# Six pairs of seven products instead of five, and bank sums put in front at a block's end

## The chip, the core and the metric

The kernel runs on one core of a Trainium2 chip. The metric is the device time of one execution in microseconds (us), the median over runs. The profile is of one execution. The engines are TensorE (PE, with its weight load PEld), VectorE (DVE), ScalarE (ACT), GpSimd (POOL) and SyncE (SP), whose queue issues the transfers used here.

## The reference

Attention with a local mask for four heads and a strided mask for four, over 8 batches of 576 tokens, gives x of 4608 tokens x 512. Then:

```python
h = x @ w_in            # 512 -> 2048
g = h * np.cos(h)
return (g @ w_out).astype(np.float32)   # 2048 -> 512
```

All is float32. The kernel multiplies in the type fp32r: each factor is split into a rounded high part and the low part that is left, and a product takes three matmuls (high x high, high x low, low x high).

## The kernel before

The first half of the time goes to attention and to h, batch by batch, where h is written to DRAM as `h_all`. The change is in the second half, the output stage. It works through 18 blocks of 256 tokens (`s`), and in each through 8 pairs (`f`) of 128-row slices of w_out. One step of the stage is a pair (s, f): `gate` makes the factors of the pair from h, and `Outputs.pair` multiplies them with the weights into banks of PSUM.

A pair is multiplied in one of two ways. A plain pair takes four products of 128 x 128 by 512 columns, 12 matmuls. A pair of seven takes seven products of 128 x 128 by 256 columns in Strassen's manner, 21 matmuls; for it the gate is extended by sums (`g[:, 4]` to `g[:, 7]`) and the weights by sums made beforehand (`output_sums`, `split_sums`). `SEVEN` lists the pairs of seven, of which block 1 uses only the first three (the length of `SUMMED`); block 0 is all plain, and so is the last block before. `ROWS` names the pairs whose weights lie in the tiles laid out for whole rows of 512 columns.

A gate goes through these steps: load h (`h_in`, from SP's queue); ScalarE writes k to `wave` (PSUM) and VectorE the remainder `r` (line 655); ScalarE takes the sine (line 657) and VectorE the product with h (line 664 or 673); for a pair of seven GpSimd then makes three sums (lines 674, 675, 678); ScalarE casts the high part `g_hi` (line 183), and `rest`, GpSimd or VectorE, subtracts it to give the low part `g_lo` (line 184). `LEADS` says how many pairs ahead of its multiplication each step of a plain pair or of a pair of seven is emitted. `BY_VECTOR` names the plain pairs whose low part VectorE makes; their product is written back to `wave`, so that one input of the subtraction lies in PSUM. For the other plain pairs the product goes to `r` in SBUF, and GpSimd subtracts. All of GpSimd's instructions for gates are chained in the order of the pairs (`by_gpsimd`).

Pairs of seven gather parts that the two halves of the output share in the banks `more` and `most`. After the last pair of seven, `shared` copies one half of `more` on ScalarE (line 746) and forms the sums on VectorE (lines 747, 749, 752), in two steps behind pairs 6 and 7. `store` adds them to the banks `lower` and `upper` (line 761; in blocks without pairs of seven it copies, line 768) and sends the rows out. Five banks are used in turn. The order of the instructions on each engine is otherwise written down by a planner from its own estimates; `order` adds a constraint of order without a wait.

Of the kernel before, what the change touches and what calls it, by code (L numbers as in the profile page):

```python
# [13 lines left out]
F32 = mybir.dt.float32  # L14
# [4 lines left out]
AF = mybir.ActivationFunctionType  # L19
ALU = mybir.AluOpType  # L20
# [6 lines left out]
P = 128  # L27
# [52 lines left out]

TB = 2 * P
NTB = NTOK // TB
SEVEN = (4, 5, 6, 1, 2)
ROWS = (0, 3, 7)


LEADS = ((6, 4, 3, 2), (7, 4.5, 3.5, 2))
AHEAD = tuple(PER_BATCH - n for n in (20, 17, 13, 10, 7, 3))

BY_VECTOR = (0, 3, 7)  # L90


SUMMED = (14, 28, 36)
# [9 lines left out]
def attention_cos_ffn(ctx, tc, qkl, vl, qkvs, w_in, w_out, eye, eye16, mask_l0, mask_l, mask_s, out):  # L103
    nc = tc.nc
# [18 lines left out]
    w_all = dram.tile([NFC, P, DM], F32, name="w_all")  # L123
    t_all = dram.tile([len(SEVEN), P, 2 * DM], F32, name="t_all")

# [8 lines left out]
    def order(later, first, reason):  # L134
        tc.add_manual_dep(
            later.ins, first.ins.name,
            mybir.DependencyInfo(mybir.DependencyClass.NoSync, mybir.DependencyReason.DATA), reason=reason,
        )
# [12 lines left out]
    def with_product(begun):  # L151
        if turn is not None:
            order(begun, turn, "with this product")

    def weight_tile(f):
        pool, n = (by_rows, len(ROWS)) if f in ROWS else (wp, NF - len(ROWS))
        return pool.tile([P, 2, 2, 2 * P], F32R, name="w", bufs=2 * n)
# [8 lines left out]
    def to_float32(raw, out, bits=None):  # L166
# [12 lines left out]
            out=out, in0=top, scalar=3, in1=bits, op0=ALU.logical_shift_left, op1=ALU.bitwise_or  # L179
        )  # L180

    def split(x, hi, lo, cast=nc.scalar.copy, rest=nc.gpsimd):
        with_product(cast(out=hi, in_=x))  # L183
        return rest.tensor_tensor(out=lo, in0=x, in1=hi.bitcast(F32), op=ALU.subtract)  # L184

    wi, whole = [], []

# [410 lines left out]
    def output_sums(cv, n):  # L598

        f = SEVEN[n]  # L600
        both = whole_tile(cv).rearrange("p (f n) -> p f n", f=2)
# [12 lines left out]
    def split_sums(room, n):  # L614
# [6 lines left out]
        split(t[:, :3], most[:, 0], most[:, 1])  # L621
        sums[SEVEN[n]] = [(most[:, 0, n], most[:, 1, n]) for n in range(3)]
        yield
# [3 lines left out]
        split(t[:, 3], *last)  # L627
        sums[SEVEN[n]].append(last)
        yield
# [1 line left out]
    wo, lasts, gates, sums = [], [], {}, {}  # L631

    def seven(s, f):
        return 0 < s < NTB - 1 and f in SEVEN[:len(SUMMED) if s == 1 else len(SEVEN)]

    of_gates = []

    def by_gpsimd(begun):
        if of_gates:
            order(begun, of_gates[-1], "pair by pair")  # L640
        of_gates.append(begun)

    def gate(s, f):

        h = hp.tile([P, 2 * TB], F32, name="h_in")
        nc.sync.dma_start(
            out=h.rearrange("p (f t) -> p f t", f=2),
            in_=h_all[2 * f:2 * f + 2, :, s * TB:(s + 1) * TB].rearrange("f p t -> p f t"),
        )
        yield  # L650
        r = rp.tile([P, 2 * TB], F32, name="r")
        wave = sg.tile([P, 2 * TB], F32, name="wave")
        k = wave.bitcast(I32)
        with_product(nc.scalar.activation(out=k, in_=h, func=AF.Copy, scale=1.0 / (2.0 * math.pi), bias=0.25))  # L654
        nc.vector.scalar_tensor_tensor(out=r, in0=k, scalar=-2.0 * math.pi, in1=h, op0=ALU.mult, op1=ALU.add)  # L655
        yield
        sin = nc.scalar.activation(out=wave, in_=r, func=AF.Sin, bias=quarter)  # L657
        with_product(sin)
        if s == 0 and f == 0:
            order(sin, exps[-1], "one change of tables")  # L660
        pool = nc.gpsimd
        if not seven(s, f):
            low, pool = (wave, nc.vector) if f in BY_VECTOR else (r, nc.gpsimd)
            nc.vector.tensor_tensor(out=low, in0=wave, in1=h, op=ALU.mult)
            yield
            g_hi, g_lo = (gp.tile([P, 7 * P], F32R, name=name) for name in ("g_hi", "g_lo"))
            lo = split(low, g_hi[:, :4 * P], g_lo[:, :4 * P], rest=pool)
            if pool is nc.gpsimd:
                by_gpsimd(lo)
            gates[s, f] = g_hi, g_lo  # L670
            yield
        g = gs.tile([P, 8, P], F32, name="g")
        nc.vector.tensor_tensor(out=g[:, :4].rearrange("p n t -> p (n t)"), in0=wave, in1=h, op=ALU.mult)
        by_gpsimd(pool.tensor_tensor(out=g[:, 4], in0=g[:, 0], in1=g[:, 2], op=ALU.add))
        by_gpsimd(pool.tensor_tensor(  # L675
            out=g[:, 5:7], in0=g[:, 0:5:4], in1=g[:, 1:2].broadcast_to([P, 2, P]), op=ALU.subtract
        ))
        by_gpsimd(pool.tensor_tensor(out=g[:, 7], in0=g[:, 3], in1=g[:, 6], op=ALU.subtract))  # L678
        yield
        g_hi, g_lo = (gp.tile([P, 7 * P], F32R, name=name) for name in ("g_hi", "g_lo"))  # L680
        by_gpsimd(split(g[:, 1:].rearrange("p n t -> p (n t)"), g_hi, g_lo))
        gates[s, f] = g_hi, g_lo
        yield

# [8 lines left out]
    class Outputs:  # L693
# [48 lines left out]
        def shared(self):  # L742

            more, most = self.banks["more"], self.banks["most"]
            self.t = op.tile([P, 5, 2 * P], F32, name="t")
            with_product(nc.scalar.copy(out=self.t[:, 0], in_=more[:, 0]))
            nc.vector.tensor_tensor(out=self.t[:, 4], in0=more[:, 1], in1=self.t[:, 0], op=ALU.add)
            yield
            nc.vector.tensor_tensor(
                out=self.t[:, 1:3], in0=most, in1=self.t[:, 4:5].broadcast_to([P, 2, 2 * P]), op=ALU.add  # L750
            )
            nc.vector.tensor_tensor(out=self.t[:, 3], in0=most[:, 0], in1=self.t[:, 2], op=ALU.add)
            yield

        def store(self):

            rows = out[self.s * TB:(self.s + 1) * TB, :].rearrange("(h p) d -> h p d", h=2)
            for half, name in enumerate(("lower", "upper")):
                o = op.tile([P, 2, 2 * P], F32, name="o", bufs=4)
                if "more" in self.banks:  # L760
                    nc.vector.tensor_tensor(
                        out=o, in0=self.banks[name], in1=self.t[:, 2 - 2 * half:4 - 2 * half], op=ALU.add
                    )
                parts = (slice(0, 1), slice(1, 2)) if self.last and half else (slice(0, 2),)
                for i, part in enumerate(parts):
                    if "more" not in self.banks:
                        copy = nc.scalar.copy if half == i else nc.vector.tensor_copy
                        copy(out=o[:, part], in_=self.banks[name][:, part])
                    nc.sync.dma_start(
                        out=rows[half].rearrange("p (n d) -> p n d", n=2)[:, part], in_=o[:, part]  # L770
                    )
# [10 lines left out]
    with ExitStack() as phase:  # L782
# [5 lines left out]
        banks = {  # L788
            name: phase.enter_context(
                tc.tile_pool(name=f"ps_{name}", bufs=bufs, space=bass.MemoryType.PSUM, reuse_waits="tile")  # L790
            ) for name, bufs in (("m", 3), ("n", 1), ("o", 1))
        }
# [8 lines left out]
        m, n, o = ((pools[name], name) for name in "mno")  # L801
# [35 lines left out]
        begun = np.interp(range(UNITS, B * UNITS + 3), [k for k, _ in KNOTS], [at for _, at in KNOTS])  # L837
        begun = begun.astype(int).tolist()
        bursts, turns = {}, {}
        waiting = {True: [], False: []}  # L840
        for n, at in enumerate(begun):
            k = n + UNITS
# [11 lines left out]
        for f in range(NF):  # L854
            first = FirstBlock(f)
            for slot in range(STEP):
                plan[STEP * f + slot] = partial(first.products, slot)
        for i, (b, f) in enumerate(itertools.product(range(1, B), range(NF)), NF):
            block = Block(b, f)
# [18 lines left out]
        for n in range(NFC - LATE):  # L878
            at = (B - 1) * PER_BATCH + STEP * (n // 2) + 12 + 3 * (n % 2)
            in_steps(output_weights(lambda: whole_tile(cv)[:, :DM], n), at - 6, at)  # L880
        for n, f in enumerate(SEVEN):
            at = 2 * PER_BATCH + 17 * (2 * f + 2)
# [12 lines left out]
        for slot in range(max(*plan, *steps) + 1):  # L895
# [9 lines left out]
            if b == B - 1:  # L905
                if at == 0:
                    attention.close()
                    sg = ctx.enter_context(tc.tile_pool(
                        name="sg", bufs=3, space=bass.MemoryType.PSUM, side="right", reuse_waits="tile"
# [10 lines left out]

    op = ctx.enter_context(tc.tile_pool(name="op", bufs=2, reuse_waits="tile"))
    tp = ctx.enter_context(tc.tile_pool(name="tp", bufs=1, reuse_waits="tile"))
    gs = ctx.enter_context(tc.tile_pool(name="gs", bufs=3, reuse_waits="tile"))
    pools = {"q": ctx.enter_context(
        tc.tile_pool(name="ps_q", bufs=1, space=bass.MemoryType.PSUM, reuse_waits="tile")
    )}
# [2 lines left out]
    for n in range(NFC - LATE, NFC):  # L929
        rest = nc.vector if n % 2 else nc.gpsimd  # L930
# [8 lines left out]
    for i, (s, f) in enumerate(tiles):  # L939
        if f == 0:  # L940
            block = Outputs(s)
        ahead(i)
        for step in made.get(i, ()):
            next(step, None)
        block.pair(f, *gates.pop((s, f)), partial(ahead, i + 0.5))
        if "more" in block.banks and f >= max(SEVEN):
            if f == max(SEVEN):
                shared = block.shared()
            next(shared, None)
        if f == NF - 1:  # L950
            block.store()

# [93 lines left out]
```

## Time and profile before

| what | value |
|---|---|
| median of 3 runs | 858.97 us (857.16 to 859.54) |
| the profiled execution | 857.26 us, its span 855.5 us |
| granted TensorE clock, mean | 0.998 of 2.4 GHz |
| TensorE busy | 845.1 us, 99% of the span |
| VectorE, ScalarE, GpSimd busy | 66%, 62%, 63% |

The span goes from the first to the last instruction. Busy shares are means over stages with different limits; matmuls are pipelined, so the distance from one start to the next says more than a duration. Line numbers are those of the kernel before.

### The profile page before, as it was taken

To read this page: it belongs to the slowest core of one execution; us is meant where nothing else is said; L and a number is where in the kernel's file an instruction comes from. 1 tells how busy PE (TensorE), PEld (TensorE's weight loads), DVE (VectorE), ACT (ScalarE), POOL (GpSimd) and SP (SyncE) were. 2 spreads that over 40 slices of the span, in tenths; PEclk is the share of its full clock that TensorE was granted. 3 is DMA by queue.
4 is the path that set the end of the run, shared out by engine and by line. 5 is a ranking of instruction groups with operands and counts; after the bars stand their busy time and mean duration, and the time that the engine had idled before them with its cause. 6 is when DMAs were issued, how large, how long until landed. Compare 5 with 4: busy or idle time off the path is not lost.

```text
span 855.5 us, 23160 instructions
## 1 busy us (share of the span) xinstructions
PE 845.1 (99%) x9147; PEld 785.3 (92%) x9147; DVE 567.4 (66%) x1087; ACT 528.4 (62%) x1031; POOL 539.7 (63%) x543
## 2 busy tenths in 40 slices
PE   9999999999999999999999999999999999999998
PEld 5799999999998999999999889999999999999996
DVE  5888755768658567676333667777777677767671
ACT  3766545545445354454456887777777777777772
POOL 2578984416207134162166478999899989898951
PEclk9999999999999999999999999999999999999999
DMA  9698444566666667665456844444444444444330
GB/s 333 189 297 296 145 163 165 178 214 207 224 222 208 230 222 226 227 213 210 155 195 222 280 135 129 131 124 125 129 131 124 132 128 124 134 126 136 120 127 26
DMA packets 91901, 151.82 MB, mean 177 GB/s; under 512 B 8464, under 2 KB 53008, under 8 KB 91792
## 3 DMA queue, kind: packets, MB, share of 16 engines
q1 hardware_dynamic: 91072, 150.11, 53.8%
q8 instruction: 72, 1.18, 0.6%
q14 instruction: 37, 0.30, 0.1%
q10 hardware_dynamic: 720, 0.23, 0.1%
HBM read 96.30 MB, written 54.00 MB: 176 GB/s over the span
## 4 chain that ended last, share of the span: by engine, by line
PE 90%; POOL 3%; ACT 2%; DVE 2%; DMA 1%; issue 1%; DVEq 0%; ACTq 0%; POOLq 0%
PE q L709 44%; PE m L532 19%; PE n L532 9%; PE o L532 5%; PE m L503 4%; PE acc L335 2%; PE acc L400 2%; PE acc L318 2%; POOL x_lo L184 2%; PE acc L387 1%; PE acc L811 1%; PE acc L370 1%; DMA h_all<-h 1%; DMA w_all<-sums 1%; PE m L370 0%
## 5 line engine op out<-in xcount | busy, mean ns | idle before, releaser
L709 PE MATMUL q<-w,g_hi 128*128 128x512 f32 (+1 forms) x1000 | 199.9, 338 | 0.0
L709 PEld LDWEIGHTS q<-w,g_hi 128*128 128x128 f32 x1000 | 159.7, 188 | 22.1
L184 POOL TENSOR_TENSOR g_lo<-g,g_hi 128x896 fp32r<-128x896 f32 x78 | 165.1, 2132 | 6.3 <-ACT g_hi L183 6.0
L709 PE MATMUL q<-w,g_lo 128*128 128x512 f32 (+1 forms) x500 | 111.4, 337 | 0.0
L532 PE MATMUL m<-x_hi,v 128*128 128x288 f32 x448 | 109.4, 299 | 0.8 <-ACT m L540 0.8
L532 PE MATMUL m<-x_hi,w 128*128 128x288 f32 x448 | 108.5, 298 | 0.4 <-DVE h L550 0.4
L655 DVE SCALAR_TENSOR_TENSOR r<-wave,h_in 128x512 f32<-128x512 int32 x144 | 96.1, 685 | 15.2 <-ACT wave L654 13.8
L657 ACT ACTIVATE wave<-r,quarter 128x512 f32<-128x512 f32 x144 | 98.6, 688 | 5.9 <-DVE r L655 5.9
L183 ACT CAST g_hi<-g 128x896 fp32r<-128x896 f32 x78 | 73.4, 941 | 39.6 <-POOL g L678 27.7
L709 PEld LDWEIGHTS q<-w,g_lo 128*128 128x128 f32 x500 | 82.7, 188 | 10.9
L654 ACT ACTIVATE wave<-h_in 128x512 int32<-128x512 f32 x144 | 83.6, 591 | 7.6 <-DVE g_lo L184 7.4
L709 PE MATMUL q<-v,g_hi 128*128 128x256 f32 x624 | 85.4, 279 | 0.0
L532 PEld LDWEIGHTS m<-x_hi,v 128*128 128x128 f32 x448 | 78.1, 188 | 2.1 <-ACT m L540 1.3
L532 PEld LDWEIGHTS m<-x_hi,w 128*128 128x128 f32 x448 | 78.0, 188 | 1.4 <-DVE h L550 0.7
L709 PEld LDWEIGHTS q<-v,g_hi 128*128 128x128 f32 x624 | 78.3, 188 | 0.0
L288 POOL TENSOR_TENSOR pn_s<-e_sb,z 128x324 f32<-128x324 f32 x28 | 20.9, 748 | 90.2 <-DVE z L286 84.0
L184 DVE TENSOR_TENSOR g_lo<-wave,g_hi 128x512 fp32r<-128x512 f32 x54 | 37.2, 689 | 53.2 <-PE q L709 36.0
L540 ACT COPY m<-m 128x288 f32<-128x288 f32 x112 | 44.5, 397 | 43.7 <-PE m L532 37.0
L288 POOL TENSOR_TENSOR e_sb<-e_sb,z 128x384 f32<-128x384 f32 x24 | 20.3, 844 | 77.6 <-DVE z L286 77.2
L532 PE MATMUL m<-x_lo,v 128*128 128x288 f32 x224 | 66.1, 295 | 0.0
L532 PE MATMUL m<-x_lo,w 128*128 128x288 f32 x224 | 65.9, 294 | 0.0
L675 POOL TENSOR_TENSOR g<-g 128x256 f32<-128x256 f32 x78 | 57.7, 740 | 6.1
(137 smaller groups left out, 2051.8 us busy)
## 6 DMA issues: line engine op xcount, KB each, us to landing
h_all<-h SPq DMA_DIRECT2D x128, 288.0 KB, 2.9
h_in<-h_all SPq DMA_DIRECT2D x144, 256.0 KB, 2.8
qk<-in_qkvs SPq DMA_DIRECT2D x28, 324.0 KB, 4.4
out<-o SPq DMA_DIRECT2D x35, 256.0 KB, 3.0
qk<-in_qkl SPq DMA_DIRECT2D x21, 416.0 KB, 4.4
raw<-in_w_in SPq DMA_DIRECT2D x16, 512.0 KB, 5.3
raw<-in_w_out SPq DMA_DIRECT2D x16, 512.0 KB, 4.8
v<-in_vl SPq DMA_DIRECT2D x24, 224.0 KB, 4.0
```

The source lines that it names most:

```text
L183: with_product(cast(out=hi, in_=x))
L184: return rest.tensor_tensor(out=lo, in0=x, in1=hi.bitcast(F32), op=ALU.subtract)
L288: nc.gpsimd.tensor_tensor(out=pn, in0=e, in1=z[:, :n].unsqueeze(2).broadcast_to([P, n, w]), op=ALU.mult)
L318: self.scored = self.pe(nc.tensor.matmul(s_ps[quarter_of(c), t * KW:(t + 1) * KW], q_t[half(j), p, QB * t:QB * (t + 1)], k_t[half(j), p, Q ...
L503: in_turn(nc.tensor.matmul(self.banks[i, j], a[:, c * P:(c + 1) * P], y[:, c], start=k == 0 and m == 0, stop=k == 1 and m == len(ops) - 1, ...
L532: in_turn(nc.tensor.matmul(bank, a[:, c * P:(c + 1) * P], y[:, c], start=first and i == 0, stop=i == len(ops) - 1, skip_group_check=True,))
L540: nc.scalar.copy(out=t, in_=self.bank[name[0]])
L654: with_product(nc.scalar.activation(out=k, in_=h, func=AF.Copy, scale=1.0 / (2.0 * math.pi), bias=0.25))
L655: nc.vector.scalar_tensor_tensor(out=r, in0=k, scalar=-2.0 * math.pi, in1=h, op0=ALU.mult, op1=ALU.add)
L657: sin = nc.scalar.activation(out=wave, in_=r, func=AF.Sin, bias=quarter)
L675: by_gpsimd(pool.tensor_tensor(out=g[:, 5:7], in0=g[:, 0:5:4], in1=g[:, 1:2].broadcast_to([P, 2, P]), op=ALU.subtract))
L709: in_turn(nc.tensor.matmul(at, a, w, start=first, stop=True, skip_group_check=True))
```

## The change

Pair 3 joins `SEVEN`, which has then six of eight pairs, and leaves `ROWS`; the last block uses pairs of seven as well. `BY_VECTOR` becomes (1, 3, 4, 6) and holds for pairs of seven too: of the six, VectorE makes the low parts of 1, 3, 4 and 6 from `g` and `g_hi`, GpSimd those of 2 and 5. The plain pairs 0 and 7 give their low parts to GpSimd. The three sums of each pair of seven stay on GpSimd. The leads of pairs of seven grow from (7, 4.5, 3.5, 2) to (8, 5.5, 4.5, 2), and `g` gets a fourth buffer. `shared` emits its copy and all its sums behind the last pair of seven (pair 6), and `then` holds every later k, sine, cast, remainder, product and VectorE low part of a gate behind them on its engine. `store` adds in parts, so that the last block can send its last half in two.

```diff
-SEVEN = (4, 5, 6, 1, 2)
-ROWS = (0, 3, 7)
+SEVEN = (4, 5, 6, 1, 2, 3)
+ROWS = (0, 7)
-LEADS = ((6, 4, 3, 2), (7, 4.5, 3.5, 2))
+LEADS = ((6, 4, 3, 2), (8, 5.5, 4.5, 2))
-BY_VECTOR = (0, 3, 7)
+BY_VECTOR = (1, 3, 4, 6)
...
+    emptied = {}
+
+    def then(engine, begun):
+        if engine in emptied:
+            order(begun, emptied[engine], "banks first")
+        return begun
+
     def split(x, hi, lo, cast=nc.scalar.copy, rest=nc.gpsimd):
-        with_product(cast(out=hi, in_=x))
-        return rest.tensor_tensor(out=lo, in0=x, in1=hi.bitcast(F32), op=ALU.subtract)
+        with_product(then("act", cast(out=hi, in_=x)))
+        begun = rest.tensor_tensor(out=lo, in0=x, in1=hi.bitcast(F32), op=ALU.subtract)
+        return then("dve", begun) if rest is nc.vector else begun
...
     def seven(s, f):
-        return 0 < s < NTB - 1 and f in SEVEN[:len(SUMMED) if s == 1 else len(SEVEN)]
+        return 0 < s and f in SEVEN[:len(SUMMED) if s == 1 else len(SEVEN)]
...
         pool = nc.gpsimd
+        rest = nc.vector if f in BY_VECTOR else pool
         if not seven(s, f):
-            low, pool = (wave, nc.vector) if f in BY_VECTOR else (r, nc.gpsimd)
-            nc.vector.tensor_tensor(out=low, in0=wave, in1=h, op=ALU.mult)
+            low = wave if f in BY_VECTOR else r
+            then("dve", nc.vector.tensor_tensor(out=low, in0=wave, in1=h, op=ALU.mult))
             yield
             g_hi, g_lo = (gp.tile([P, 7 * P], F32R, name=name) for name in ("g_hi", "g_lo"))
-            lo = split(low, g_hi[:, :4 * P], g_lo[:, :4 * P], rest=pool)
-            if pool is nc.gpsimd:
+            lo = split(low, g_hi[:, :4 * P], g_lo[:, :4 * P], rest=rest)
+            if rest is pool:
                 by_gpsimd(lo)
...
-        by_gpsimd(split(g[:, 1:].rearrange("p n t -> p (n t)"), g_hi, g_lo))
+        lo = split(g[:, 1:].rearrange("p n t -> p (n t)"), g_hi, g_lo, rest=rest)
+        if rest is pool:
+            by_gpsimd(lo)
...
-            with_product(nc.scalar.copy(out=self.t[:, 0], in_=more[:, 0]))
+            emptied["act"] = then("act", nc.scalar.copy(out=self.t[:, 0], in_=more[:, 0]))
+            with_product(emptied["act"])
             nc.vector.tensor_tensor(out=self.t[:, 4], in0=more[:, 1], in1=self.t[:, 0], op=ALU.add)
-            yield
...
-            nc.vector.tensor_tensor(out=self.t[:, 3], in0=most[:, 0], in1=self.t[:, 2], op=ALU.add)
-            yield
+            emptied["dve"] = nc.vector.tensor_tensor(
+                out=self.t[:, 3], in0=most[:, 0], in1=self.t[:, 2], op=ALU.add
+            )
...
-                if "more" in self.banks:
-                    nc.vector.tensor_tensor(
-                        out=o, in0=self.banks[name], in1=self.t[:, 2 - 2 * half:4 - 2 * half], op=ALU.add
-                    )
                 parts = (slice(0, 1), slice(1, 2)) if self.last and half else (slice(0, 2),)
                 for i, part in enumerate(parts):
-                    if "more" not in self.banks:
+                    if "more" in self.banks:
+                        nc.vector.tensor_tensor(
+                            out=o[:, part], in0=self.banks[name][:, part],
+                            in1=self.t[:, 2 - 2 * half:4 - 2 * half][:, part], op=ALU.add,
+                        )
+                    else:
...
-    gs = ctx.enter_context(tc.tile_pool(name="gs", bufs=3, reuse_waits="tile"))
+    gs = ctx.enter_context(tc.tile_pool(name="gs", bufs=4, reuse_waits="tile"))
...
-        if "more" in block.banks and f >= max(SEVEN):
-            if f == max(SEVEN):
-                shared = block.shared()
-            next(shared, None)
+        if "more" in block.banks and f == max(SEVEN):
+            block.shared()
```

The remaining lines of the diff put `then` around the k, sine, remainder and product of `gate` in the same way.

## Rows read from the trace of the kernel before

**Rows 1.** The page: busy time, share of the span and instructions of each engine.

```profile
PE 845.1 (99%) x9147; PEld 785.3 (92%) x9147; DVE 567.4 (66%) x1087; ACT 528.4 (62%) x1031; POOL 539.7 (63%) x543
```

**Rows 2.** TensorE in time: start, us, line, operation, matmuls; block 6, 7, the last.

```profile
601.32 2.01 PE L709 MATMUL q<-w,g_hi 128*128 128x512 f32 x8
...
604.09 1.98 PE L709 MATMUL q<-w,g_hi 128*128 128x512 f32 x8
...
606.81 0.86 PE L709 MATMUL q<-w,g_hi 128*128 128x256 f32 x6
...
611.71 2.00 PE L709 MATMUL q<-w,g_hi 128*128 128x512 f32 x8
...
614.45 0.86 PE L709 MATMUL q<-w,g_hi 128*128 128x256 f32 x6
...
639.03 0.51 PE L709 MATMUL q<-w,g_lo 128*128 128x256 f32 x3
...
641.48 0.51 PE L709 MATMUL q<-w,g_lo 128*128 128x256 f32 x3
...
840.52 2.03 PE L709 MATMUL q<-w,g_hi 128*128 128x512 f32 x8
...
843.32 2.03 PE L709 MATMUL q<-w,g_hi 128*128 128x512 f32 x8
```

**Rows 3.** One block: us, then PE, PEld, DVE, ACT, POOL busy us (instructions), clock, DMA.

```profile
621.81:642.29 20.48, 20.48 (x143) 19.01 (x142) 14.70 (x25) 16.10 (x26) 18.65 (x21) 1.00 0.42 129
```

**Rows 4.** GpSimd in time, in that block: start, us, line, operation.

```profile
627.87 0.46 POOL L674 TENSOR_TENSOR g<-g 128x128 f32<-128x128 f32 x1
628.40 0.74 POOL L675 TENSOR_TENSOR g<-g 128x256 f32<-128x256 f32 x1
629.22 0.46 POOL L678 TENSOR_TENSOR g<-g 128x128 f32<-128x128 f32 x1
629.64 0.46 POOL L674 TENSOR_TENSOR g<-g 128x128 f32<-128x128 f32 x1
...
635.27 4.21 POOL L184 TENSOR_TENSOR g_lo<-g,g_hi 128x896 fp32r<-128x896 f32 x2
639.42 0.47 POOL L674 TENSOR_TENSOR g<-g 128x128 f32<-128x128 f32 x1
```

**Rows 5.** Groups by form from 380 us on: count, busy us, mean ns, idle before.

```profile
L184 POOL TENSOR_TENSOR g_lo<-g,g_hi 128x896 fp32r<-128x896 f32 x78 | 165.1, 2132 | 6.3 <-ACT g_hi L183 6.0
...
L184 POOL TENSOR_TENSOR g_lo<-r,g_hi 128x512 fp32r<-128x512 f32 x12 | 15.7, 1307 | 21.1 <-ACT g_hi L183 11.1 <-PE q L709 10.0
...
L184 DVE TENSOR_TENSOR g_lo<-wave,g_hi 128x512 fp32r<-128x512 f32 x54 | 37.2, 689 | 53.2 <-PE q L709 36.0 <-POOL g_lo L184 17.0
...
L752 DVE TENSOR_TENSOR t<-q,t 128x256 f32<-128x256 f32 x16 | 6.8, 424 | 0.5
```

**Rows 6.** VectorE and GpSimd together, 93 to 97 us: DVE, then POOL, then forms.

```profile
93.60 1.97 DVE L469 TENSOR_TENSOR t<-x,x 128x576 f32<-128x576 f32 x1 [1.09 <-POOL x_lo L184]
...
93.52 1.43 POOL L184 TENSOR_TENSOR x_lo<-x,x_hi 128x576 fp32r<-128x576 f32 x1
94.92 2.37 POOL L184 TENSOR_TENSOR v<-sums,v 128x768 fp32r<-128x768 f32 x1
...
L469 DVE TENSOR_TENSOR t<-x,t x14: 741/1214/1969, 90.2 to 432.2; 128x576 f32<-128x576 f32 x14
...
L184 POOL TENSOR_TENSOR v<-sums,v x8: 1856/1868/2377, 60.0 to 132.4; 128x768 fp32r<-128x768 f32 x8
```

**Rows 7.** VectorE in time, two products without a gap.

```profile
628.17 1.28 DVE L673 TENSOR_TENSOR g<-wave,h_in 128x512 f32<-128x512 f32 x2
```

**Rows 8.** Waits from 520 us on: us in total, times, longest.

```profile
ACT g_hi L183 <- PE q L709: 36.7, 74, 1.9
```

**Rows 9.** The last instructions in time, on VectorE and ScalarE.

```profile
851.93 0.42 DVE L768 COPY o<-q 128x256 f32<-128x256 f32 x1 [7.65 <-PE q L709]
852.39 0.37 ACT L768 COPY o<-q 128x256 f32<-128x256 f32 x1 [1.29 <-DVE o L768]
```

More of the change, by code (lines that the diff above doesn't have):

```diff
@@ L653, in gate @@
         k = wave.bitcast(I32)
-        with_product(nc.scalar.activation(out=k, in_=h, func=AF.Copy, scale=1.0 / (2.0 * math.pi), bias=0.25))
-        nc.vector.scalar_tensor_tensor(out=r, in0=k, scalar=-2.0 * math.pi, in1=h, op0=ALU.mult, op1=ALU.add)
+        with_product(then("act", nc.scalar.activation(
+            out=k, in_=h, func=AF.Copy, scale=1.0 / (2.0 * math.pi), bias=0.25
+        )))
+        then("dve", nc.vector.scalar_tensor_tensor(
+            out=r, in0=k, scalar=-2.0 * math.pi, in1=h, op0=ALU.mult, op1=ALU.add
+        ))
         yield
         sin = nc.scalar.activation(out=wave, in_=r, func=AF.Sin, bias=quarter)
-        with_product(sin)
+        with_product(then("act", sin))
         if s == 0 and f == 0:
@@ L672, in gate @@
         g = gs.tile([P, 8, P], F32, name="g")
-        nc.vector.tensor_tensor(out=g[:, :4].rearrange("p n t -> p (n t)"), in0=wave, in1=h, op=ALU.mult)
+        then("dve", nc.vector.tensor_tensor(
+            out=g[:, :4].rearrange("p n t -> p (n t)"), in0=wave, in1=h, op=ALU.mult
+        ))
         by_gpsimd(pool.tensor_tensor(out=g[:, 4], in0=g[:, 0], in1=g[:, 2], op=ALU.add))
```

## Prediction, written before the changed kernel was run

> **What bounds the kernel now.** The page comes first: TensorE is busy for 845.1 us of the 855.5 us span, the other engines for about two thirds [rows 1]. A busy TensorE says little by itself, so TensorE's timeline in the output stage comes next. Pairs there start at a fixed beat. In blocks 2 to 16 the plain pairs 7, 0 and 3 last 2.77, 2.72 and 2.74 us (601.32 to 604.09 to 606.81, and 611.71 to 614.45), and a pair of seven products lasts 2.45 us (two of them from 606.81 to 611.71) [rows 2]. The sum over a block is 5 x 2.45 + 2.77 + 2.72 + 2.74 = 20.48 us, which is also the length of the window in which TensorE is busy for 20.48 us at a granted clock of 1.00 [rows 3]. So TensorE alone sets the time of these blocks, and any matmul time removed is gained as long as the gates keep coming.
>
> The same window says who makes the gates: GpSimd is busy for 18.65 of 20.48 us, ScalarE for 16.10, VectorE for 14.70 [rows 3]. GpSimd is the next limit. The waits show that the makers are ahead: casts of gates wait for TensorE to give a g_hi tile back, 36.7 us in 74 waits [rows 8].
>
> **What TensorE gains.** Pair 3 goes from plain to seven: 2.74 - 2.45 = 0.29 us in each of blocks 2 to 16, so 4.35 us. In block 17 six plain pairs become sevens. A plain pair whose weights are not in the row tiles lasts 2.80 us there (840.52 to 843.32) [rows 2], so 6 x 0.35 = 2.10 us. Pair 3 leaves the row tiles and stays plain in blocks 0 and 1, where I charge it 2.80 instead of 2.74 us: 0.12 us. Together TensorE loses 6.33 us of work, and a block of the steady stretch comes to 20.48 - 0.29 = 20.19 us.
>
> **What the gates cost GpSimd.** From start to start, the three sums of one pair take 1.77 us (627.87 to 629.64) and a low part of 896 columns takes 2.08 us (635.27 to 639.42, two of them) [rows 4]. Before, that is 5 x (1.77 + 2.08) = 19.25 us of a block. After, six pairs have sums (10.62), the low parts of pairs 2 and 5 stay (4.16), and those of the plain pairs 0 and 7 come to GpSimd: their recorded 1.307 us [rows 5], less the 0.04 by which recorded ends overlap the next start, is 1.27 each (2.54). That is 17.32 us, well below 20.19.
>
> But the low parts of pairs 1, 3, 4 and 6 now run on VectorE with both inputs, g and g_hi, in SBUF. Before, VectorE's low parts read the wave from PSUM and took 689 ns in all 54 cases [rows 5]. No instruction of this form at 896 columns is in the trace. From 424 ns at 256 columns and 689 ns at 512 [rows 5] an estimate is 1.09 us, or 1.01 us from start to start (two products of 512 take 1.28 us, so 0.08 is overlap) [rows 7]. What such an instruction does to GpSimd is seen in the attention stage. The subtraction of line 469, with two SBUF inputs of 576 columns, takes 0.741 us at best and 1.214 in the median. At 93.60 it takes 1.97 us: GpSimd's low part runs until 94.95, and the GpSimd instruction that starts at 94.92 takes 2.37 instead of 1.86 us [rows 6]. The two take turns: VectorE waited for the one GpSimd instruction, and the next lost 0.51 us to VectorE.
>
> So GpSimd pays for the moved low parts too. Of the 0.741 us at 576 columns it lost 0.51, that is 0.23 less than the duration; at 1.09 us that makes 0.86. Where VectorE's turn falls into one of the gaps of about 0.08 us between the three dependent sums [rows 4] the loss is nearer 0.78. I take 0.80, since GpSimd spends over half of its time in low parts; 0.76 and 0.86 are the ends, and nothing at all if GpSimd happens to be idle. GpSimd with its turns then needs 17.32 + 4 x 0.80 = 20.52 us for each block, and TensorE gives it 20.19. It falls 0.33 us behind per block, 4.95 us over the 15 blocks whose gates have successors.
>
> **What hides that.** The lead of the gates: a low part ends at 639.48 where TensorE takes it at 641.48, and the one ahead of it at about 637.4 for 639.03 [rows 2, 4]. So 1.6 us is the cover, and the rest stops TensorE: 4.95 - 1.6 = 3.35 us. The longer leads and the fourth g tile let sums start earlier, but g_hi tiles are still three, so I give them no more cover.
>
> **VectorE and ScalarE.** VectorE's 14.70 us [rows 3] lose three low parts of 512 (0.60 each) and gain four of 1.01: 16.94 us. To this comes the time behind GpSimd, 1.214 - 0.741 = 0.47 each in the median of line 469 [rows 6], so 18.8 of 20.19 us: hidden, with 1.4 us to spare. ScalarE gains one wider cast, under half a microsecond on 16.10 [rows 3]: hidden under TensorE.
>
> **The block's end.** The copy and the three sums of banks are held in front of later casts, sines, products and VectorE low parts. Behind them wait all of ScalarE's and VectorE's later gate work, until TensorE has finished pair 6. TensorE itself waits for none of it before, since pairs 7 and 0 run without a gap [rows 2]. I cost this at nothing: TensorE has two pairs, 5.49 us, before it needs pair 1's gate, and the chain that it waits behind is some 2 us. With that cover gone it is a rival below.
>
> **The rest at nothing.** The extra sums of weights for pair 3 fall into the batches that TensorE bounds; the third load of sums into a ring of two tiles waits for the split at pairs 6 and 7 and is needed only at pair 19, and if it held SP's queue the tile loads behind it would be late. The tail: the last two copies, 0.42 us on VectorE and then 0.37 on ScalarE [rows 9], become two VectorE sums of 256 columns, 0.42 each: no more than 0.1 us either way.
>
> **The sum.** -6.33 + 3.35 = -2.98 us. The profiled execution took 857.26 us (span 855.5), so 854.3 by that one. The median of the three runs is 858.97, and I forecast against it: 856.0.
>
> **The rivals.** *All of it hidden.* If VectorE's turns fall where GpSimd would have waited anyway (it still idles about 1.2 us of a block before: 20.48 - 19.25), nothing of the 6.33 us is lost: 852.6. Against it stands the sum of 20.52. *VectorE runs out.* This is the one on the other side. It decides when a moved low part waits over (20.19 - 16.94) / 4 = 0.81 us for GpSimd. The longest wait at line 469 is 1.969 - 0.741 = 1.23 us, the low parts of GpSimd in this stage are longer (2132 ns [rows 5]), and each block's end now makes VectorE wait for TensorE and ScalarE. With 0.9 us per wait and 0.6 us at the block's end a block takes 16.94 + 3.6 + 0.6 = 21.1 us: 0.9 x 15 - 1.6 = 11.9 us of stalls, so +5.6 and 864.6. For it speaks that VectorE works strictly in order; against it the 0.47 of the median. *GpSimd loses the whole of each VectorE instruction.* Then it is 4 x 1.09 = 4.36 us, 21.68 per block, 1.49 x 15 - 1.6 = 20.8 us of stalls and 873.4. Against it stands the loss of 0.51 at 0.741 us. The Trainium skill, page SBUF — State Buffer, section Who interferes with whom, has the rule that would do this: a VectorE instruction with two SBUF inputs and a GpSimd instruction that reads SBUF exclude each other, and whichever is first holds the port for its whole instruction. By that rule the trace agrees on the turns (1.97 us for 0.741) but shows a smaller loss than the whole. *The order at the block's end costs.* If the gates held behind it come 0.3 us late at each of 16 ends, the chain's 2 us less the cover of 1.6, that adds 4.8 to the forecast: 860.8.
>
> **How the numbers follow.** Forecast 0.43, all hidden 0.24, VectorE 0.21, whole instruction 0.04, block's end (with SP's queue) 0.08. The forecast's own range comes from the ends of the turn's price: at 0.76, 20.36 per block leaves 0.95 us of stalls and 853.6; at 0.86, 20.76 leaves 6.95 and 859.6. The range of 8 in 10 reaches from just under the all-hidden case, 852.3, to 863.5, which leaves out the upper half of the VectorE case and what is above it. A measurement of this kernel tells about 0.3% from no change, 2.6 us, so faster ends at 856.4. Faster: all hidden and half of the forecast, 0.46. Same: the forecast's other half and part of the block's end, 0.26. Slower: 0.28.
>
> **What would show it.** Right: 99 pairs of seven at 2.45 us; VectorE's low parts of 896 columns with a median well over 1.09 us and a spread up to about 3; some GpSimd sums and low parts longer by about 0.8 us, where they did not vary before; GpSimd without idle time in the later blocks, and TensorE's first gaps only after some four or five blocks, in front of the low products. Wrong: a block beat of 20.19 to the end (turns hidden), or gaps from block 2 on with VectorE the busiest engine. The prediction fails most easily on the price of a turn, since 0.06 us of it moves the result by 3.6 us.

## The result, and the profile after

The changed kernel takes 869.46 us (median of 4 runs, 868.1 to 871.82) against 858.69 for the kernel before (4 runs), a ratio of 1.0127 with a 95% interval of 1.0106 to 1.0148. It is 10.8 us slower. The forecast was 856.0, the range 852.3 to 863.5; slower had a chance of 0.28. The profiled execution took 869.32 us, its span 867.5.

The page after, its busy shares and two of its lines of 40 slices (tenths of each slice, 21.7 us long):

```profile
PE 846.2 (98%) x9336; PEld 791.4 (91%) x9336; DVE 654.2 (75%) x1110; ACT 534.7 (62%) x1032; POOL 559.1 (64%) x593
...
DVE  5888756758667576676324679999999999999996
...
POOL 2578974316126242262365598888888888888885
```

TensorE has 1.1 us more busy time than before [rows 1] in a span 12 us longer. Its counted work is 6.3 us less, so part of its waiting must stand in these records as busy time; in the run without turns below it is busy for 838.8 us. In the output stage VectorE is at 9 tenths or more in each of 15 slices, up to the last but one. It would be easy to stop here and call VectorE the new bound.

TensorE in time (start, length, line, operation, matmuls merged, idle before and its releaser):

```profile
522.79 1.98 PE L726 MATMUL q<-w,g_hi 128*128 128x512 f32 x8
...
542.96 1.97 PE L726 MATMUL q<-w,g_hi 128*128 128x512 f32 x8
...
563.13 1.98 PE L726 MATMUL q<-w,g_hi 128*128 128x512 f32 x8
...
567.35 0.74 PE L726 MATMUL q<-v,g_hi 128*128 128x256 f32 x4 [0.17 <-DVE o L781]
...
571.08 0.62 PE L726 MATMUL q<-w,g_lo 128*128 128x256 f32 x3 [0.54 <-POOL g_lo L191]
...
592.53 0.62 PE L726 MATMUL q<-w,g_lo 128*128 128x256 f32 x3 [0.54 <-POOL g_lo L191]
```

The first three lines are the starts of pair 0 of blocks 2, 3 and 4: the beat is 20.17 us, as counted, where [rows 2] gave 20.48. The stalls begin in block 4, and from then on the wait for `g_lo` of pair 2 comes back every 592.53 - 571.08 = 21.45 us. One block of that stretch, in the columns of [rows 3]:

```profile
635.48:656.93 21.45, 20.73 (x151) 19.37 (x151) 19.78 (x26) 16.04 (x25) 18.88 (x23) 1.00 0.40 124
```

VectorE went from 14.70 to 19.78 us of a block that is now 21.45 us long, GpSimd from 18.65 to 18.88. TensorE is recorded as busy for 20.73 us, where blocks 2 and 3, with the same matmuls, took 20.17 in all.

GpSimd in time, over one beat of that stretch (compare [rows 4]):

```profile
635.35 1.34 POOL L689 TENSOR_TENSOR g<-g 128x128 f32<-128x128 f32 x1
...
637.58 1.19 POOL L693 TENSOR_TENSOR g<-g 128x128 f32<-128x128 f32 x1
638.73 0.46 POOL L689 TENSOR_TENSOR g<-g 128x128 f32<-128x128 f32 x1
...
640.50 2.13 POOL L191 TENSOR_TENSOR g_lo<-g,g_hi 128x896 fp32r<-128x896 f32 x1
644.27 0.46 POOL L689 TENSOR_TENSOR g<-g 128x128 f32<-128x128 f32 x1 [1.63 <-DVE g L686]
...
650.34 1.31 POOL L689 TENSOR_TENSOR g<-g 128x128 f32<-128x128 f32 x1
...
656.83 1.32 POOL L689 TENSOR_TENSOR g<-g 128x128 f32<-128x128 f32 x1
```

A sum of 128 columns takes 0.46 us when nothing is in its way, as at 638.73; those into which a turn of VectorE falls take 1.34, 1.19 and 1.31 in this beat, and the 1.32 at 656.83 opens the next one. Before, all of them were alike (means of 465 and 461 ns). And in front of the sum at 644.27 GpSimd is idle for 1.63 us. VectorE at the same time:

```profile
636.89 1.55 DVE L191 TENSOR_TENSOR g_lo<-g,g_hi 128x896 fp32r<-128x896 f32 x1
...
641.76 1.83 DVE L191 TENSOR_TENSOR g_lo<-g,g_hi 128x896 fp32r<-128x896 f32 x1
643.51 0.68 DVE L686 TENSOR_TENSOR g<-wave,h_in 128x512 f32<-128x512 f32 x1
...
654.84 2.98 DVE L191 TENSOR_TENSOR g_lo<-g,g_hi 128x896 fp32r<-128x896 f32 x1
```

This is where the idle time comes from. VectorE reaches pair 6's low part at 641.76, but GpSimd is in its own low part until 642.63, so VectorE gets its turn only then and ends at 643.59. The product that GpSimd's next sum needs (643.51, line 686) stands behind that low part on VectorE and ends at 644.19. So GpSimd lost the rest of VectorE's low part and the whole product: 0.96 + 0.60, and the way of the signal. It is the largest wait of GpSimd in this stage, once per block (us in total, times, longest):

```profile
POOL g L689 <- DVE g L686: 24.8, 16, 1.6
...
PE q L726 <- POOL g_lo L191: 7.5, 14, 0.6
```

All 66 low parts of VectorE with two inputs in SBUF (shortest, median, longest, ns), where those of 512 columns that read the wave from PSUM took 689 in the mean [rows 5] (the mean of these 66 is 1870):

```profile
L191 DVE TENSOR_TENSOR g_lo<-g,g_hi x66: 1149/1694/2985, 508.2 to 856.1; 128x896 fp32r<-128x896 f32 x66
```

### The profile page after: what moved, and what is told of

Read it like the earlier page. It is cut to its first block, busy times and chain, and to the rows that moved or that the text cites. A ratio compares the mean times of both kernels' runs of the same rounds, so it can differ in the third digit from the quotient of the medians.

```text
span 867.5 us, 23572 instructions
## 1 busy us (share of the span) xinstructions
PE 846.2 (98%) x9336; PEld 791.4 (91%) x9336; DVE 654.2 (75%) x1110; ACT 534.7 (62%) x1032; POOL 559.1 (64%) x593
## 4 chain that ended last, share of the span: by engine, by line
PE 52%; DVE 15%; ACT 13%; issue 9%; POOL 6%; DMA 3%; DVEq 0%; SPq 0%; ACTq 0%; POOLq 0%
PE m L540 18%; PE n L540 9%; PE q L726 9%; PE m L511 4%; PE o L540 4%; ACT g_hi L190 4%; DVE g L686 4%; DVE r L665 4%; ACT wave L662 4%; DVE g_lo L191 3%; ACT wave L669 3%; PE acc L343 2%; PE acc L408 2%; POOL x_lo L191 2%; PE acc L326 1%
## 5 line engine op out<-in xcount | busy, mean ns | idle before, releaser
L726 PE MATMUL q<-w,g_hi 128*128 128x256 f32 (+1 forms) x958 | 175.9, 321 | 0.0
L191 DVE TENSOR_TENSOR g_lo<-g,g_hi 128x896 fp32r<-128x896 f32 x66 | 123.4, 1870 | 2.8 <-ACT g_hi L190 1.4
L190 ACT CAST g_hi<-g 128x896 fp32r<-128x896 f32 x99 | 92.5, 935 | 53.3 <-POOL g L693 53.2
L726 PE MATMUL q<-v,g_hi 128*128 128x256 f32 x792 | 112.5, 281 | 2.2 <-DVE o L781 1.7
L726 PE MATMUL q<-w,g_lo 128*128 128x256 f32 (+1 forms) x479 | 101.1, 324 | 7.5 <-POOL g_lo L191 7.5
L726 PEld LDWEIGHTS q<-v,g_hi 128*128 128x128 f32 x792 | 100.6, 188 | 5.0 <-DVE o L781 5.0
L689 POOL TENSOR_TENSOR g<-g 128x128 f32<-128x128 f32 x99 | 72.8, 736 | 24.8 <-DVE g L686 24.8
L690 POOL TENSOR_TENSOR g<-g 128x256 f32<-128x256 f32 x99 | 73.4, 741 | 7.7
L191 POOL TENSOR_TENSOR g_lo<-g,g_hi 128x896 fp32r<-128x896 f32 x33 | 70.2, 2128 | 0.0
L686 DVE TENSOR_TENSOR g<-wave,h_in 128x512 f32<-128x512 f32 x99 | 67.3, 680 | 3.1 <-ACT wave L669 2.9
```

The costliest lines, as they stand in the source:

```text
L190: with_product(then("act", cast(out=hi, in_=x)))
L191: begun = rest.tensor_tensor(out=lo, in0=x, in1=hi.bitcast(F32), op=ALU.subtract)
L686: then("dve", nc.vector.tensor_tensor(out=g[:, :4].rearrange("p n t -> p (n t)"), in0=wave, in1=h, op=ALU.mult))
L690: by_gpsimd(pool.tensor_tensor(out=g[:, 5:7], in0=g[:, 0:5:4], in1=g[:, 1:2].broadcast_to([P, 2, P]), op=ALU.subtract))
L726: in_turn(nc.tensor.matmul(at, a, w, start=first, stop=True, skip_group_check=True))
```

## The experiments

Each is an edit of the changed kernel, but for the eighth, which is one of the kernel before.

**No turns.** VectorE's low part reads one input from SBUF instead of two.

```diff
-        begun = rest.tensor_tensor(out=lo, in0=x, in1=hi.bitcast(F32), op=ALU.subtract)
+        if rest is nc.vector and lo.shape[1] == 7 * P:
+            nc_low = nc.allow_low_precision(reason="one input")
+            with nc_low:
+                begun = rest.tensor_reduce(out=lo, in_=hi.bitcast(F32).unsqueeze(2), op=ALU.add, axis=AX.X)
+        else:
+            begun = rest.tensor_tensor(out=lo, in0=x, in1=hi.bitcast(F32), op=ALU.subtract)
```

> This kernel is the changed one, but VectorE makes the low parts of 896 columns as a reduction over axes of length one that reads g_hi alone, so with one SBUF input instead of two; their values are then g_hi and not the difference. The number of columns and the instruction's place stay. Theory of turns (VectorE and GpSimd exclude each other while VectorE reads two SBUF inputs, and the waits fill VectorE): the low parts take about 1.1 us each without spread, GpSimd's sums are 0.46 us throughout, the block beat falls from 21.45 to 20.2 us and the time to about 852 to 854. Theory of the block's end (copies and sums in front stop the engines): the beat stays above 21 us and the time above 865. Theory of the r tile (plain low parts on GpSimd hold it): the time stays above 861.

Measured: 852.04 us, a ratio of 0.9916 (0.9894 to 0.9939). The groups of VectorE's low parts and of GpSimd's sums, and TensorE at pair 7 of two blocks:

```profile
L194 DVE TENSOR_REDUCE g_lo<-g_hi 128x896 fp32r<-128x896 f32 x66 | 71.4, 1081 | 13.9 <-ACT g_hi L190 11.9
...
L698 POOL TENSOR_TENSOR g<-g 128x128 f32<-128x128 f32 x99 | 45.8, 463 | 7.6
L694 POOL TENSOR_TENSOR g<-g 128x128 f32<-128x128 f32 x99 | 45.7, 462 | 43.0 <-DVE g L691 43.0
```

```profile
602.56 2.00 PE L731 MATMUL q<-w,g_hi 128*128 128x512 f32 x8
...
622.72 2.00 PE L731 MATMUL q<-w,g_hi 128*128 128x512 f32 x8
```

The low parts take 1.08 us in the mean, the sums 0.46, and the beat is 20.16 us. So the rest of what the change adds to GpSimd and VectorE costs nothing; the second SBUF input costs 869.46 - 852.04 = 17.4 us. The measured 852.04 is close to the 852.6 that was forecast for the case that all is hidden.

**The order at the block's end, and the r tile.**

```diff
     def then(engine, begun):
-        if engine in emptied:
-            order(begun, emptied[engine], "banks first")
         return begun
```

> The changed kernel without the order that puts the copy and sums of banks in front of later gate work. Theory of turns: within 3 us of the changed kernel's 869.5, since VectorE has the same work and the same waits. Theory of the block's end: below 864, and VectorE's idle time at the block's end goes.

```diff
-(("gp", 3), ("hp", 5), ("rp", 3))
+(("gp", 3), ("hp", 5), ("rp", 4))
```

> The changed kernel with four r tiles instead of three. In the changed kernel VectorE's remainder waits 0.55 us per block for GpSimd's plain low part to give r back. Theory of turns: at most these 0.55 us in 14 blocks, so not below 862. Theory of the r tile: the wait was also holding up the sines behind it, and the time falls below 860.

Measured: 869.48 us (1.0122, 1.0103 to 1.0141) and 868.79 us (1.0125, 1.0106 to 1.0143). Neither makes a difference. Waits without the order:

```profile
POOL g L687 <- DVE g L684: 24.6, 15, 1.8
...
PE q L724 <- DVE t L763: 12.8, 13, 1.0
```

GpSimd's idle time is as before; TensorE now waits for the sums of banks, which the order had brought forward, instead of for pair 2's low part. The order moves a wait that another line causes.

**Three turns, the plain pairs back.**

```diff
-BY_VECTOR = (1, 3, 4, 6)
+BY_VECTOR = (0, 1, 4, 6, 7)
```

> The changed kernel with BY_VECTOR = (0, 1, 4, 6, 7): three low parts of pairs of seven on VectorE instead of four, and the plain pairs 0 and 7 on VectorE again, read from the wave in PSUM. Theory of turns: GpSimd has 10.62 + 3 x 2.08 = 16.9 us and three turns of 0.8, so 19.3; VectorE 16.94 - 1.01 + 2 x 0.61 = 17.2 and three waits of 0.8, so 19.6; both are below 20.19, and the time falls to 853 to 858. Theory of the block's end: above 864.

Measured: 885.99 us (1.0322, 1.0302 to 1.0342), a miss by 28 us and on the wrong side. Waits, and TensorE at pair 0 of two blocks:

```profile
POOL g L689 <- DVE g L686: 47.4, 33, 2.0
...
DVE g L686 <- POOL g_lo L191: 25.5, 16, 1.6
```

```profile
611.53 1.98 PE L726 MATMUL q<-w,g_hi 128*128 128x512 f32 x8
...
633.89 1.98 PE L726 MATMUL q<-w,g_hi 128*128 128x512 f32 x8
```

The beat is 22.36 us, though the sums of busy time and turns were below 20.19 for both engines. VectorE's product now waits for GpSimd's low part, which gives back the tile for g (16 times, up to 1.6 us), and GpSimd then waits for that product, 47.4 us in all. The two low parts of pairs 2 and 3 follow close on each other on GpSimd here. That this neighbourhood is the cause is read from the waits and was not tried. What the beat is made of can be read from GpSimd's long sums and idle times in one block:

```profile
612.89 1.19 POOL L693 TENSOR_TENSOR g<-g 128x128 f32<-128x128 f32 x1
615.04 0.47 POOL L689 TENSOR_TENSOR g<-g 128x128 f32<-128x128 f32 x1 [0.96 <-DVE g L686]
...
622.75 1.30 POOL L689 TENSOR_TENSOR g<-g 128x128 f32<-128x128 f32 x1
...
627.46 1.32 POOL L689 TENSOR_TENSOR g<-g 128x128 f32<-128x128 f32 x1
...
632.13 0.46 POOL L689 TENSOR_TENSOR g<-g 128x128 f32<-128x128 f32 x1 [1.99 <-DVE g L686]
```

The three turns cost 0.73, 0.84 and 0.86 us, about what was said. The expectation left out the waits for products, 0.96 and 1.99 us: 10.62 + 3 x 2.08 + 2.43 + 2.95 = 22.24 us, against the beat of 22.36.

**Two turns.** The one-input form for pairs 3 and 6 alone:

```diff
+ONE_INPUT = (3, 6)
...
-        lo = split(g[:, 1:].rearrange("p n t -> p (n t)"), g_hi, g_lo, rest=rest)
+        lo = split(g[:, 1:].rearrange("p n t -> p (n t)"), g_hi, g_lo, rest=rest, one=f in ONE_INPUT)
```

> The changed kernel with one SBUF input (the reduction over g_hi, values not the difference) in the low parts of pairs 3 and 6 alone; pairs 1 and 4 keep two inputs, so there are two turns per block instead of four. If the stall begins only when VectorE is full (19.8 us busy and 1.65 idle of 21.45 with four turns of 0.79 us waiting), two turns leave VectorE 18.2 + 1.65 = 19.9 us, under 20.19: 852 to 854, as with no turn. If every turn costs TensorE alike, half of the 17.4 us between none and four remains: 860 to 861.

Measured: 852.97 us, 0.9943 (0.9929 to 0.9958). Two turns are hidden, four are not: the cost is not so much per turn, it begins where some line is full. The run does not say which, and one of the two turns that it takes away is pair 6's, the one with the 1.63 us.

**Which engine's line.** Take about the same time from the one and from the other, and leave all four turns.

```diff
-                        nc.vector.tensor_tensor(
-                            out=o[:, part], in0=self.banks[name][:, part],
-                            in1=self.t[:, 2 - 2 * half:4 - 2 * half][:, part], op=ALU.add,
-                        )
+                        nc.scalar.copy(out=o[:, part], in_=self.banks[name][:, part])
```

> The changed kernel with the two output tiles of a block copied by ScalarE instead of summed by VectorE, so that the shared sums are left out of the output. VectorE loses 2 x 0.6 = 1.2 us per block, ScalarE gains 1.2, the four turns stay. If VectorE's line of work sets the beat of 21.45: down by 1.1 to 1.2 us, 852 to 856. If GpSimd's loss in the turns sets it: no lower than 866.

```diff
-            out=g[:, 5:7], in0=g[:, 0:5:4], in1=g[:, 1:2].broadcast_to([P, 2, P]), op=ALU.subtract
+            out=g[:, 5:8], in0=g[:, 4:5].broadcast_to([P, 3, P]), in1=g[:, 1:2].broadcast_to([P, 3, P]),
+            op=ALU.subtract,
         ))
-        by_gpsimd(pool.tensor_tensor(out=g[:, 7], in0=g[:, 3], in1=g[:, 6], op=ALU.subtract))
```

> The changed kernel with GpSimd's second and third sum of a pair made by one instruction of 384 columns, with other values than the sums of the factors. GpSimd loses about 0.2 us per pair, 1.2 us per block, as much as VectorE loses in the run beside it; the four turns stay. If VectorE's line sets the beat: within 4 us of 869.5. If GpSimd sets it: down by 1.2 us in 14 blocks, 852 to 856.

Measured: 871.15 us with less on VectorE (1.0157, 1.0139 to 1.0174), 852.33 us with less on GpSimd (0.994, 0.9926 to 0.9954). With less on VectorE, a stretch of 20.5 us (columns of [rows 3]) and GpSimd in time:

```profile
640.50:661.00 20.50, 19.46 (x144) 18.27 (x143) 16.48 (x22) 17.00 (x27) 18.01 (x22) 1.00 0.44 128
```

```profile
635.49 1.22 POOL L693 TENSOR_TENSOR g<-g 128x128 f32<-128x128 f32 x1
...
638.74 1.31 POOL L689 TENSOR_TENSOR g<-g 128x128 f32<-128x128 f32 x1
...
643.15 2.13 POOL L191 TENSOR_TENSOR g_lo<-g,g_hi 128x896 fp32r<-128x896 f32 x1
646.91 0.47 POOL L689 TENSOR_TENSOR g<-g 128x128 f32<-128x128 f32 x1 [1.63 <-DVE g L686]
...
653.00 1.31 POOL L689 TENSOR_TENSOR g<-g 128x128 f32<-128x128 f32 x1
...
656.99 1.23 POOL L693 TENSOR_TENSOR g<-g 128x128 f32<-128x128 f32 x1
```

VectorE is now busy for 16.48 of 20.5 us, far from full (ScalarE, which took the copies, for 17.00), and nothing is gained: GpSimd idles the same 1.63 us before the same sum, and the turns cost the same 0.76 to 0.85. With less on GpSimd, its two sums, and the same stretch:

```profile
L690 POOL TENSOR_TENSOR g<-g 128x384 f32<-128x384 f32 x99 | 109.4, 1105 | 7.7
L689 POOL TENSOR_TENSOR g<-g 128x128 f32<-128x128 f32 x99 | 75.0, 757 | 33.5 <-DVE g L686 33.5
```

```profile
640.50:661.00 20.50, 20.50 (x155) 19.54 (x154) 19.47 (x26) 16.88 (x26) 18.40 (x18) 1.00 0.44 134
```

VectorE is as busy as in the changed kernel (19.47 us), each turn is still there (the first sum's mean is 757 ns instead of 465), and TensorE has no gap. So GpSimd's line sets the beat, and a VectorE at 9 tenths was no bound.

**The last block alone**, on the kernel before.

```diff
-        return 0 < s < NTB - 1 and f in SEVEN[:len(SUMMED) if s == 1 else len(SEVEN)]
+        return 0 < s and f in SEVEN[:len(SUMMED) if s == 1 else len(SEVEN)]
```

> The kernel before with one part of the change alone: pairs of seven in the last block too, five of eight, and the last half stored in two sums. TensorE loses 5 x 0.35 = 1.75 us, GpSimd keeps the load that it has in every block before, no VectorE instruction reads two SBUF inputs. All theories: 857.1, a ratio of 0.998; what would speak against the count of TensorE is a ratio of 1 or above.

Measured: 857.38 us, 0.9991 (0.9982 to 1.0000), so 0.998 lies just outside the interval and a ratio of 1 at its end: by the time alone the run neither confirms nor refutes the count. In its profile the last block goes from 831.42 to 852.1, 20.7 us instead of 22.5, which is the gain that was counted. The output stage started at 480.7 us there and at 478.7 in the profile of before; where the first half lost these 2 us is open, but the stage started between 477.3 and 482.0 in the profiles of this study.

**The product ahead of the low part.** Pair 1's remainder, sine and product are emitted one pair earlier, so that on VectorE the product stands in front of pair 6's low part.

```diff
+EARLY = (8, 6.5, 5.5, 2)
...
-            if i - at in LEADS[seven(*tile)]:
+            if i - at in (EARLY if seven(*tile) and tile[1] == 1 else LEADS[seven(*tile)]):
```

> The changed kernel with the remainder, sine and product of pair 1, where it is a pair of seven, emitted one pair earlier, so that on VectorE this product stands ahead of pair 6's low part instead of behind it. All four turns stay. Theory of GpSimd's line (its instructions and what it loses in the turns add up to the beat, and one of the turns costs 1.63 us because GpSimd's next sum needs a product queued behind VectorE's low part): this turn costs about 0.8 like the others, the beat goes from 21.45 to 20.6, and with a cover of 1.6 us the time to about 857. If that idle time is only a symptom of another line: 866 or more.

Measured: 858.57 us (0.9991, 0.9978 to 1.0005). GpSimd, and TensorE at pair 7 of two blocks that lie three apart:

```profile
636.73 2.13 POOL L192 TENSOR_TENSOR g_lo<-g,g_hi 128x896 fp32r<-128x896 f32 x1
638.81 1.31 POOL L690 TENSOR_TENSOR g<-g 128x128 f32<-128x128 f32 x1
...
657.39 2.14 POOL L192 TENSOR_TENSOR g_lo<-g,g_hi 128x896 fp32r<-128x896 f32 x1
```

```profile
621.82 2.01 PE L727 MATMUL q<-w,g_hi 128*128 128x512 f32 x8
...
683.84 2.01 PE L727 MATMUL q<-w,g_hi 128*128 128x512 f32 x8
```

Behind the low part of 636.73 the sum starts at once, at 638.81, and the turn now costs 1.31 - 0.46 = 0.85 us like the others. The beat is (683.84 - 621.82) / 3 = 20.67 us here, and the next low part of this pair starts 657.39 - 636.73 = 20.66 later; 20.6 was expected. One product moved forward on VectorE, with its remainder and sine, takes 869.46 - 858.57 = 10.9 us from the changed kernel, and 14 blocks with 1.63 - 0.85 us less on GpSimd's line make as much.

**A plain low part off GpSimd**, without and with the early product.

```diff
-BY_VECTOR = (1, 3, 4, 6)
+BY_VECTOR = (0, 1, 3, 4, 6)
```

> The changed kernel with the plain pair 0 back on VectorE, read from the wave in PSUM: BY_VECTOR = (0, 1, 3, 4, 6). GpSimd loses 1.27 us per block, VectorE gains 0.6, the four turns stay. Theory of GpSimd's line: the beat goes to 20.2, the time to 852 to 855. If VectorE's load decides: 869 or more. The run with three low parts shows what could spoil it: a wait of VectorE for a tile that GpSimd's low part holds.

> Both of the edits beside it: pair 1's product early and plain pair 0 on VectorE. Theory of GpSimd's line: 17.3 - 1.27 + 4 x 0.8 = 19.3 us, below TensorE's 20.19, so the time is that without turns, about 852, and below the kernel before by 0.7 to 0.8%. If VectorE is full by now: 855 or more.

With the early product and pair 7 instead of pair 0, `BY_VECTOR = (1, 3, 4, 6, 7)`:

> As the run beside it, with plain pair 7 on VectorE instead of plain pair 0: BY_VECTOR = (1, 3, 4, 6, 7). The same sum for GpSimd, 19.3 us, and the same time of about 852; a difference between the two would come from the place in the block alone, where pair 7 lies next to the sums of banks on VectorE.

Measured: 855.7 us (0.9966, 0.995 to 0.9982), 852.61 us (0.9922, 0.9902 to 0.9942) and 853.63 us (0.9942, 0.9923 to 0.996). The second of them, busy shares, TensorE at pair 0 of two blocks, and one sum on GpSimd:

```profile
PE 837.2 (99%) x9336; PEld 788.8 (93%) x9336; DVE 641.1 (76%) x1128; ACT 532.4 (63%) x1032; POOL 539.3 (64%) x575
```

```profile
601.61 1.98 PE L727 MATMUL q<-w,g_hi 128*128 128x512 f32 x8
...
621.77 1.98 PE L727 MATMUL q<-w,g_hi 128*128 128x512 f32 x8
```

```profile
643.00 0.46 POOL L690 TENSOR_TENSOR g<-g 128x128 f32<-128x128 f32 x1 [1.63 <-DVE g L687]
```

The first of the three lies 0.7 us above its range: GpSimd still idles 1.63 us once per block there and 0.36 us once more, and the later blocks take 20.4 to 20.7 us. In the second the beat is 20.16 us, though VectorE still makes four low parts with two inputs per block. This version gains what the sixth pair of seven and the last block offer, and is 0.8% faster than the kernel before. But its time was forecast from 19.3 us for GpSimd, and that sum did not come true: an idle time of 1.63 us is back in most blocks, in front of another sum, and with it and the sums of 1.31, 1.19 and 1.33 us in that block GpSimd's line comes to 16.05 + 1.63 + 0.85 + 0.73 + 0.87 = 20.13 us, just under the beat. How much of this is room that TensorE's pace leaves, the runs do not show. Pairs 0 and 7 cannot be told apart, since their intervals overlap.

## Why the prediction was wrong, point by point

**TensorE's gain was right.** 6.33 us were counted; without turns the kernel measures 858.82 - 852.04 = 6.8 us below before (5.2 to 9.1 by the interval of its ratio), and its beat is 20.16 us for the counted 20.19.

**GpSimd's work was right.** It is the line that decides, as the sum had it, and the runs with less on the one engine and on the other show that. The gates fall behind until the cover is gone, and the stalls begin in front of the low products. They begin after two blocks, in block 4, and not after four or five, as the text said, since the gates lose 1.26 us per block and not 0.33. The sign "GpSimd without idle time in the later blocks" failed as well: the 1.63 us once per block are idle time, and they were the clue.

**The step that failed is the price of a turn: "I take 0.80, since GpSimd spends over half of its time in low parts; 0.76 and 0.86 are the ends".** Three of the four turns cost about what was said: 1.34 - 0.46 = 0.88, 1.19 - 0.46 = 0.73 and 1.31 - 0.46 = 0.85 us. The lower end of 0.76 has no working in the text, where the figure for a gap is 0.78; it decides nothing here. The fourth turn costs 1.63, because GpSimd could not go on when VectorE's low part was through: its next sum needed a product queued behind that low part. With the work as counted, 17.32 + 0.88 + 0.73 + 1.63 + 0.85 = 21.41 us, and the beat is 21.45. Put into the text's own sum, 21.45 - 20.19 = 1.26 us for 15 blocks less the cover of 1.6 makes 17.3 us of stalls, and -6.33 + 17.3 = +11.0; measured is +10.8. The range missed it because its upper end priced a turn by its length alone. The text asked what is queued behind the order at the block's end, but not behind the low part on VectorE, where the answer was in the order of emission: pairs 7 and 0 are plain and have no sums, so that after pair 5's low part GpSimd's next work is pair 1's sums, whose product is emitted behind pair 6's low part. The trace of before had a wait of this kind in nearly every block, while GpSimd still had room for it, and the sum put it at nothing (from 520 us on):

```profile
POOL g L674 <- DVE g L673: 9.6, 15, 1.1
```

**"VectorE runs out" was the wrong rival, though it ended on the right side.** It named 0.9 us of waiting per low part and 864.6 us. The waits are not much shorter (a mean of 1870 ns where 1090 was estimated, so 0.78 us), and VectorE stands at 9 tenths. But VectorE relieved by 1.2 us leaves the time where it is, and VectorE as full as that beside a relieved GpSimd gives 852.33.

**"GpSimd loses the whole of each VectorE instruction" does not hold.** The plain turns cost 0.73 to 0.88 us of a low part of 1.09, and that its 873.4 us lies nearest to the measured time is luck. The Trainium skill, page SBUF — State Buffer, section SBUF: two separate sides, has the rule that whichever of the two instructions starts first keeps the shared pair of ports for the whole instruction. The trace agrees that the one waits for the other's whole instruction (VectorE's low parts last up to 2985 ns), while what the engine behind loses is less than the instruction's length. *All hidden* fell by the result; it is what two turns or none give.

**The order at the block's end was rightly costed at nothing**, and so were the third load of sums, which no wait of TensorE names, and the tail: the last two sums take 0.76 us together at 863.76, against 0.42 and 0.37 with a gap between them [rows 9].

## What to carry to other kernels

When two engines take turns at something, the price of a turn for the one that bounds is the other's turn plus whatever the first needs next that is queued behind it: look in both queues at what comes after the contended instruction, and move the producer in front of it. A busy share of 9 tenths on an engine that spends part of it waiting inside its instructions does not make it the bound; take a little work from each candidate and see which one moves the time. And where sums of busy time are a few per cent from the beat, they forecast neither side: the run with three turns had both sums below the beat and was 3% slower, by the idle time behind the turns that neither sum held.

## What the runs showed of the hardware that was not expected

Two turns per block cost nothing, and four cost 17.4 us or, with one product moved and one plain low part off GpSimd, nothing: the loss of GpSimd is swallowed whole as long as its line has room. And a low part with two inputs in SBUF can last 2985 ns on VectorE where 1.09 us is its own length (the median of 33 in the run with two turns is 1092 ns), since it waits for the end of a GpSimd low part of 2.13 us; a reduction over as many columns, with one input from SBUF, takes 1.08 us in the mean of 66.
